# Sigmoid attention and a squared-ReLU feed-forward layer on one core: the scores of whole key chunks become native float32 products in quarters of the TensorE array

## The chip, the cores and the metric

The kernel runs on one core of one Trainium2 chip. The metric is the device time of one execution in microseconds (us), taken as the median over several runs. The engines spoken of are PE (TensorE, which multiplies matrices), PEld (its loading of the stationary operand, the "weights" of a product), DVE (VectorE), ACT (ScalarE) and SP (SyncE, which here only issues DMA transfers).

## The reference

`q`, `k`, `v` have 8 batches, 12 heads, 448 positions and 64 numbers per head; the feed-forward layer has 768 inputs and 2048 hidden units. All numbers are float32.

```python
def _attn_ref(q, k, v):
    S = q.shape[2]
    scale = 1.0 / np.sqrt(q.shape[-1])
    scores = scale * np.matmul(q, k.transpose(0, 1, 3, 2)) - np.log(S)
    attn = 1.0 / (1.0 + np.exp(-scores))
    return np.matmul(attn, v).astype(np.float32)

def _moe_ref(x, w_in, w_out, s, b):
    h = x @ w_in
    r = np.maximum(h, 0.0)
    g = s * (r * r) + b
    return (g @ w_out).astype(np.float32)

def reference(**kwargs):
    ...
    attn_out = _attn_ref(**attn_kwargs)
    B, H, S, D = attn_out.shape
    x = np.ascontiguousarray(attn_out.transpose(0, 2, 1, 3)).reshape(B * S, H * D)
    return _moe_ref(x=x, **moe_kwargs)
```

## The kernel before

The program has two parts. The attention comes first and takes the first quarter of the time; the feed-forward layer follows. The feed-forward layer runs over seven groups of 512 tokens: the first one directly, the other six in two threes, each with fewer products and with sums of weights and activations that DVE and ACT make ahead of them. The change doesn't touch that part.

**Quads.** The attention is a loop over 24 quads: a batch `b` and a third `t` of the 12 heads, so four heads. They are numbered 0 to 23 here. The four heads lie as `i` (0 or 1) and a half `r` of the 128 partitions: rows 0 to 63 hold one head's 64 numbers, rows 64 to 127 the other's. The tile `qk` of a quad is 128 partitions by `[i, queries or keys, 448]`.

**Blocks of scores.** The 448 keys of a head are three whole chunks of 128 and a last one of 64. A block `(i, c)` holds the scores of one whole chunk for the two heads of `i`: keys on the 128 partitions of the output, 448 queries along the free axis, head `j` in bank `j` of a PSUM tile of two banks. A quad has six blocks. ACT makes one sigmoid (L647) of each. The last chunks of all four heads make a seventh tile, `psc_l` (L686), with two heads' 64 keys on each half of the partitions; it is made one quad ahead.

**Scores in three products.** Before the change a block is made of three products of rounded parts. `hi` is the number rounded to the format that TensorE multiplies in one pass (fp32r), `lo` is what is left; the products are hi\*hi, lo\*hi and hi\*lo (`PARTS`). The parts of a quad are made one quad ahead: ACT rounds queries and whole key chunks (`parts_hi`, L630) after the six sigmoids, and DVE subtracts (`parts_lo`, L424) after its other work of the quad. For the first two quads DVE makes both (`parts_dve`). The first two blocks of quad 0 are native float32 products of the half arrays (L671), since their parts would come too late. Each product uses 64 rows by 128 columns of the array, and the two heads of a block run side by side in the two halves.

**Attention times values.** In 23 of the 24 quads the products with `v` are native float32 products in quarters of the array (64 rows by 64 columns), four at a time (`quarters`, L729; the last chunk L741). A native float32 product is one instruction of the program and two MATMUL records in the trace, so four products are `x8`. Quad 22 has them over 128 rows by 64 columns (`attn_v`, L699).

**PSUM slots.** There are four slots of two banks. Blocks one, two, five and six and `psc_l` take turns in `turn` (0 and 1). Blocks three and four stand in `held` (2 and 3), where the two `pav` tiles of the quad before have stood, and where those of this quad will stand. `held` is reversed after each quad in quarters. What releases a `pav` tile at the end of a quad is a copy on ACT (L734), a copy on DVE (L754) and two additions on DVE (L421, one per `pav` tile), which wait for the last product of the quad (L741):

```python
    def quarters_store(b, t, pav, x, last):
        copy = nc.vector.tensor_copy(x[:, 0], pav[0][:, 1, :S])
...
        for i in range(2):
            add(x[:, i], x[:, i], pav[i][:, i, :S])
```

Before the change the third block that PE makes is `(1, 0)`, which needs the slot that the first addition frees, and the fourth is `(0, 2)`, which needs the second addition.

**Other work.** Beside this, DVE, ACT and SP prepare the weights of the feed-forward layer in pieces that are laid out over the quads by hand-set tables (`ticks`). Each engine takes its instructions strictly in the order in which the program emits them. SP's queue in a quad is: the store of the quad before (`xd`), the values of the next quad (`v`), queries and keys two quads ahead (`qk`, into the buffer that this quad's scores read), weights (`st`), sums (`wd`).

Of the kernel before, what the change touches and what calls it, by code (L numbers as in the profile page):

```python
# [12 lines left out]
F32R = mybir.dt.float32r  # L13
# [25 lines left out]
PARTS = ((0, 0), (0, 1), (1, 0))  # L39
# [9 lines left out]
LATER_SUMS = (2, 3)  # L49
LATER_DUE = ((30.0, 84.0), (86.0, 140.0))  # L50
ROLL = 7
TWO = range(1, 24)
ROOM = 1.8
ACT_JOBS, ACT_AHEAD = 1.75, 0.9
DVE_JOBS = 6.9
# [276 lines left out]
def sigmoid_attention_relu2_ffn(  # L332
# [10 lines left out]
    nc = tc.nc  # L343
    B, NQ, P, _, _, S = qk.shape
    D = v.shape[5]
    NF, _, DM = w_in.shape
# [14 lines left out]
    def pool(stack, name, bufs, side=None, space=None):  # L361
        kw = dict(side=side) if side else {}
        if space is not None:
            kw["space"] = space
        return stack.enter_context(
            tc.tile_pool(name=name, bufs=bufs, reuse_waits="tile", **kw)
        )
# [49 lines left out]
    def f32(ap):  # L417
        return ap.bitcast(F32)
# [4 lines left out]
    def sub(o, x, y):  # L423
        nc.vector.tensor_tensor(o, x, y, op=ALU.subtract)  # L424


    order = [f + h * NP for f in range(NP) for h in range(2)]
# [160 lines left out]
    ldv = pool(at, "ldv", 2)  # L588
    qkx = ExitStack()
    ld = pool(qkx, "ld", 2)  # L590
    hl = pool(qkx, "hl", 1)
    ps_qk = pool(qkx, "ps_qk", 1, space=PSUM)
    ps_av = pool(at, "ps_av", 1, space=PSUM, side="right")

    turn, held = [0, 1], [2, 3]

    def place(k, name):
        pl = ps_qk if k < 2 else ps_av
        return pl.tile([P, 2, 512], F32, tag=f"s{k}", name=name)

    half = (slice(0, D), slice(D, P))
    quads = [(b, t) for b in range(B) for t in range(NQ)]
    NL = len(quads)

    def load(b, t, first=False):
        x = ld.tile([P, 2, 2, S], F32, tag="qk", name=f"qk_{b}_{t}")
        if first:
            nc.sync.dma_start(x[:, 0, 1, :P], qk[b, t][:, 0, 1, :P])
            nc.scalar.dma_start(x[:, 0, 0], qk[b, t][:, 0, 0])
            nc.sync.dma_start(x[:, 0, 1, P:], qk[b, t][:, 0, 1, P:])  # L610
            nc.scalar.dma_start(x[:, 1, 0], qk[b, t][:, 1, 0])
            nc.sync.dma_start(x[:, 1, 1], qk[b, t][:, 1, 1])
        else:
            nc.sync.dma_start(x, qk[b, t])
        return [x]
# [3 lines left out]
        nc.sync.dma_start(vt, v[b, t])  # L619
        ld_.append(vt)  # L620

    NX = S + 3 * P

    def flat(x):
        return x.rearrange("p i x s -> p i (x s)")[:, :, :NX]

    def parts_hi(b, t, ld_):

        hi, lo = (hl.tile([P, 2, NX], F32R, tag=h, name=f"qk{h}_{b}_{t}") for h in "hl")
        nc.scalar.copy(hi, flat(ld_[0]))  # L630
        ld_.append((hi, lo))

    def parts_lo(ld_):
        hi, lo = ld_[-1]
        sub(lo, flat(ld_[0]), f32(hi))

    def parts_dve(b, t, ld_, pieces):
        hi, lo = (hl.tile([P, 2, NX], F32R, tag=h, name=f"qk{h}_{b}_{t}") for h in "hl")
        x = flat(ld_[0])
        for i, cols in pieces:  # L640
            nc.vector.tensor_copy(hi[:, i, cols], x[:, i, cols])  # L641
            sub(lo[:, i, cols], x[:, i, cols], f32(hi[:, i, cols]))
        ld_.append((hi, lo))

    def sigmoid(psc, name):
        a = ap_.tile([P, 2, S], F32, tag="a", name=f"a_{name}")
        nc.scalar.activation(a, psc[:, :, :S], AF.Sigmoid, bias=nls, scale=SCALE)  # L647
        return a

    def scores(b, t, ld_):  # L650
        x = ld_[0]
        two = ld_.pop() if len(ld_) > 2 else None
        whole = two is None or (b, t) == quads[0]
        a = {}
        psc = {}
        order = [(i, c) for i in range(2) for c in range(3)]
        if not whole:
            order[2:4] = order[3], order[2]
        for k, (i, c) in zip(turn + (held[::-1] if whole else held) + turn, order):
            o = psc[i, c] = place(k, f"psc_{b}_{t}_{i}_{c}")  # L660
            if two and (i or c == 2 or not whole):
                cols = slice(S + c * P, S + (c + 1) * P)
                for m, (wi, xi) in enumerate(PARTS):
                    for j, r in enumerate(half):
                        nc.tensor.matmul(  # L665
                            o[:, j, :S], two[wi][r, i, cols], two[xi][r, i, :S],
                            start=m == 0, stop=m == 2,
                        )
            else:
                for j, r in enumerate(half):  # L670
                    nc.tensor.matmul(  # L671
                        o[:, j, :S], x[r, i, 1, c * P : (c + 1) * P], x[r, i, 0, :],
                        start=True, stop=True,
                    )
            if not whole and (i, c) == (1, 0):
                continue
            for k in [(i, c)] + [(1, 0)] * (not whole and (i, c) == (0, 2)):
                a[k] = sigmoid(psc[k], f"{b}_{t}_{k[0]}_{k[1]}")
        return a

    def scores_last(b, t, ld_, k):
        x = ld_[0]
        psc = place(k, f"psc_{b}_{t}_l")
        for j, r in enumerate(half):
            for i in range(2):
                nc.tensor.matmul(  # L686
                    psc[half[i], j, :S], x[r, i, 1, 3 * P :], x[r, i, 0, :],
                    start=True, stop=True,
                )
        return sigmoid(psc, f"{b}_{t}_l")  # L690
# [70 lines left out]
    loaded = {0: load(*quads[0], first=True)}  # L761
# [23 lines left out]
    def ticks(n, part, upto=99.0):  # L785
        jobs = sorted(plan.pop((n, part), ()), key=lambda x: x[:2])
        while jobs and jobs[0][3] <= upto:
            upto -= jobs[0][3]
            jobs.pop(0)[2]()
        if jobs:  # L790
            plan[n, part] = jobs
# [53 lines left out]
    pieces = [(l, f + h * NQ4) for f in range(NQ4) for l in (1, 0) for h in range(4)]  # L845
# [3 lines left out]
    pieces, late = iter(pieces[:-LATE]), pieces[-LATE:]  # L849
# [54 lines left out]
    at_step(NL - 1, "END", 0, lambda: first_lo(1))  # L904
    at_step(NL - 1, "END", -1, lambda: (base_lo(0, 0, w1[0]), base_store(0, 0, w1[0])))

    parts_dve(*quads[0], loaded[0], [(0, slice(S)), (1, slice(S)), (0, slice(S + 2 * P, NX)), (1, slice(S, NX))])
    al = {}

    def last_scores(n):  # L910
        al[n] = scores_last(*quads[n], loaded[n], turn[n == 1])
        if n > 1:
            turn.reverse()

    in_quarters = [n for n in range(NL) if n == NL - 1 or act(n) <= ACT_JOBS and dve[n] <= DVE_JOBS]
    for n, (b, t) in enumerate(quads):
        if n:
            ticks(n, "DVE")
        a = scores(b, t, loaded[n])
        between = None  # L920
        if n == 0:
            parts_dve(*quads[1], loaded[1], [(i, slice(NX)) for i in range(2)])
            ticks(0, "DVE")
            firsts = []

            def between():
                firsts.append(scores_last(*quads[0], loaded[0], 0))
                ticks(0, "ACT", ACT_AHEAD)

        else:  # L930
            if n + 1 in TWO:
                parts_hi(*quads[n + 1], loaded[n + 1])
            if n in in_quarters:

                def between():
                    if n + 1 < NL:
                        last_scores(n + 1)
                    ticks(n, "ACT", ACT_AHEAD if n + 1 < NL else 2.4)

            else:  # L940
                ticks(n, "ACT", ROOM)
        if n + 2 < NL:
            loaded[n + 2] = load(*quads[n + 2])
        ticks(n, "SP")
        for fn in stores:
            fn()
        stores.clear()
        if n == NL - 1:
            qkx.close()
            ps_h = pool(blk_ps, "ps_h", 2, space=PSUM)  # L950
        pav = (quarters if n in in_quarters else attn_v)(b, t, loaded[n], a, between)
        last = al[n] if n else firsts[0]
        if n + 1 < NL and n + 1 not in al:
            last_scores(n + 1)
        ticks(n, "ACT")
        if n in in_quarters:
            q_last = quarters_last(loaded[n], last, *pav)
        else:
            attn_v_last(loaded[n], last, pav)
        if n and n + 1 in TWO:  # L960
            parts_lo(loaded[n + 1])
        ticks(n, "END")
        if n in in_quarters:
            quarters_store(b, t, *pav[:2], q_last)
        else:
            store_x(b, t, pav)
        if n + 2 < NL:
            load_v(*quads[n + 2], loaded[n + 2])
# [365 lines left out]
    for a, *_ in PRODUCTS_1:  # L1334
        seen = [a]
        while seen:
            x = seen.pop(0)
# [178 lines left out]
    o = plan1.op("SP", 0.0, readers, opened, late=OPEN_DUE)  # L1516
# [3 lines left out]
    x = None  # L1520
    for k in range(AHEAD):
        _, l, row, p = stream[k]
        after = [o, x] + [row_op.get((l, row, f)) for f in (2 * p, 2 * p + 1)]
        x = plan1.op("SP", 1.28, after, lambda at: fetch(), late=OPEN_DUE + 6.0 + 2.8 * k)
# [84 lines left out]
```

## Time and profile before

| what | before |
|---|---|
| time, median of 3 runs | 1014.2 us (1013.45 to 1015.75) |
| span of the profiled execution | 1011.5 us |
| what lies around the span (median less span) | 2.7 us |
| attention, from the start to the first product of the feed-forward layer | 246.6 us |
| busy share of the span: PE, DVE, ACT | 100%, 88%, 72% |
| granted TensorE clock | 1.000 |

The profile is of one execution. Its span runs from the first to the last instruction; the timed runs also count what lies around it, so a change of the span is added to the median. A busy PE is one with a product somewhere in its pipeline; it does not say that the products follow each other as closely as they can. That is read from the distance between the starts of products that follow each other.

### The profile page before, as it was taken

The numbers are of one execution on the slowest core, as the hardware profiler recorded it, in microseconds if no ns is written. First come the engines' busy times: TensorE is split into PE (matmuls) and PEld (weight loads), VectorE is DVE, ScalarE is ACT, GpSimd is POOL, SyncE is SP. The second block draws the span as 40 slices with busy tenths as digits, with TensorE's granted clock in tenths as the row PEclk, the third lists the DMA queues.
The fourth block names the chain that finished last, engine by engine and source line by source line (L and its number), as shares of the span: only waits on it lengthen the run. The fifth ranks groups of instructions, "written<-read, shape, count | busy, mean of one in ns | idle before, by whom it ended". The sixth has DMA issues, their size and how long they took to land.

```text
span 1011.5 us, 15098 instructions
## 1 busy us (share of the span) xinstructions
PE 1007.4 (100%) x5746; PEld 766.2 (76%) x5746; DVE 891.7 (88%) x1035; ACT 725.7 (72%) x795; POOL 0.2 (0%) x4
## 2 busy tenths in 40 slices
PE   9999999999999999999999999999999999999998
PEld 4555555556888888888888888888888888888887
DVE  5999999999999957999978999996668678899995
ACT  7999999999777756748999944424544979964430
POOL 0000000000000000000000000000000000000000
PEclk9999999999999999999999999999999999999999
DMA  8887999996998999998966666898776666666774
GB/s 304 306 317 273 357 340 393 341 354 256 357 409 333 356 397 368 363 336 276 308 190 195 197 188 192 253 357 302 216 217 190 193 199 188 191 200 191 211 249 165
DMA packets 101080, 278.87 MB, mean 276 GB/s; under 512 B 10000, under 2 KB 23184, under 8 KB 101008
## 3 DMA queue, kind: packets, MB, share of 16 engines
q1 hardware_dynamic: 100720, 277.45, 80.1%
q8 instruction: 46, 0.75, 0.3%
q10 hardware_dynamic: 288, 0.46, 0.1%
q14 instruction: 26, 0.21, 0.1%
HBM read 193.99 MB, written 83.89 MB: 275 GB/s over the span
## 4 chain that ended last, share of the span: by engine, by line
PE 99%; DMA 0%; DVE 0%; issue 0%
PE b L1091 31%; PE b L1100 31%; PE pav L729 11%; PE psc L665 9%; PE ph L881 6%; PE po L1353 6%; PE psc_l L686 2%; PE pav L741 2%; PE pav L699 0%; DMA qk<-qk_t 0%; PE o L1114 0%; DVE qkl L424 0%; DVE qkh L641 0%; PE pav L708 0%; DVE r L424 0%
## 5 line engine op out<-in xcount | busy, mean ns | idle before, releaser
L1091 PE MATMUL b<-o_0h,wu 128*128 128x512 f32 x928 | 286.1, 389 | 0.0
L1091 PEld LDWEIGHTS b<-o_0h,wu 128*128 128x128 f32 x928 | 174.2, 188 | 36.1
L1091 PE MATMUL b<-o_0l,wu 128*128 128x512 f32 x464 | 180.5, 389 | 0.0
L1100 PE MATMUL b<-o_0h,wu 128*128 128x512 f32 x464 | 152.2, 389 | 0.0
L1100 PE MATMUL b<-o_1h,wu 128*128 128x512 f32 x456 | 149.6, 389 | 0.0
L647 ACT ACTIVATE a<-psc,nls 128x896 f32<-128x896 f32 x144 | 132.9, 1009 | 7.8 <-PE psc L665 5.5
L729 PE MATMUL pav<-a,v 64*64 64x448 f32 x1104 | 113.0, 540 | 0.0
L421 DVE TENSOR_TENSOR r<-r,b 128x1024 f32<-128x1024 f32 x74 | 89.4, 1215 | 24.4 <-PE b L1091 19.1
L1091 PEld LDWEIGHTS b<-o_0l,wu 128*128 128x128 f32 x464 | 87.1, 188 | 18.0
L1100 PEld LDWEIGHTS b<-o_0h,wu 128*128 128x128 f32 x464 | 87.1, 188 | 18.1
L1100 PEld LDWEIGHTS b<-o_1h,wu 128*128 128x128 f32 x456 | 85.7, 188 | 17.7
L424 DVE TENSOR_TENSOR r<-r,b 128x1024 f32<-128x1024 f32 x66 | 79.9, 1215 | 20.4 <-PE b L1100 11.8
L1100 PE MATMUL b<-o_0l,wu 128*128 128x512 f32 x232 | 90.2, 389 | 0.0
L1100 PE MATMUL b<-o_1l,wu 128*128 128x512 f32 x228 | 88.7, 389 | 0.0
L729 PEld LDWEIGHTS pav<-a,v 64*64 64x64 f32 x1104 | 40.0, 133 | 58.8 <-issue 46.2
L1041 ACT CAST o_0h<-r 128x1024 fp32r<-128x1024 f32 x26 | 27.4, 1052 | 57.2 <-DVE r L424 35.3
L1146 ACT ACTIVATE r<-b 128x1024 f32<-128x1024 f32 x46 | 46.3, 1027 | 30.2 <-DVE r L421 12.8
L1353 PE MATMUL po<-g,w 128*128 128x512 f32 x288 | 67.7, 389 | 0.0
L494 ACT CAST t<-t 128x768 fp32r<-128x768 f32 (+2 forms) x62 | 44.7, 734 | 29.1 <-DVE t L424 19.6
L1353 PEld LDWEIGHTS po<-g,w 128*128 128x128 f32 x288 | 54.1, 188 | 11.2
L881 PE MATMUL ph<-x0h,w 128*128 128x512 f32 x192 | 61.6, 390 | 0.0
L1220 ACT ACTIVATE r<-r,b_sb,s_sb 128x1024 f32<-128x1024 f32 x48 | 59.5, 1242 | 1.0
(122 smaller groups left out, 1728.2 us busy)
## 6 DMA issues: line engine op xcount, KB each, us to landing
wu<-wd SPq DMA_DIRECT2D x232, 512.0 KB, 3.6
wd<-t SPq DMA_DIRECT2D x36, 768.0 KB, 7.6
qk<-qk_t SPq DMA_DIRECT2D x23, 896.0 KB, 7.1
st<-w_out SPq DMA_DIRECT2D x16, 768.0 KB, 8.8
st<-w_in SPq DMA_DIRECT2D x16, 768.0 KB, 8.5
wd<-t SPq DMA_DIRECT2D x22, 512.0 KB, 4.8
v<-v_t SPq DMA_DIRECT2D x24, 448.0 KB, 5.7
xd<-xo SPq DMA_DIRECT2D x24, 448.0 KB, 3.5
```

The source lines that it names most:

```text
L421: nc.vector.tensor_tensor(o, x, y, op=ALU.add)
L424: nc.vector.tensor_tensor(o, x, y, op=ALU.subtract)
L494: nc.scalar.copy(ts[g][:, :n, 0], f32(ts[g][:, :n, 1]))
L647: nc.scalar.activation(a, psc[:, :, :S], AF.Sigmoid, bias=nls, scale=SCALE)
L665: nc.tensor.matmul(o[:, j, :S], two[wi][r, i, cols], two[xi][r, i, :S], start=m == 0, stop=m == 2,)
L729: nc.tensor.matmul(o[r, m, :S], ld_[1][rows, 3 * i + c, j, :], a[i, c][rows, j, :], start=c == 0, stop=c == 2 and m != i,)
L881: nc.tensor.matmul(ph, w[:, k, wi, kc * P : (kc + 1) * P], x0[h][xi][:, cc, :], start=m == 0, stop=m == 3 * NCC - 1,)
L1091: nc.tensor.matmul(bk[:, j], wt[:, j, wi, c * P : (c + 1) * P], tiles[xi][:, c, :], start=first and m == 0, stop=m == 3 * KC - 1, skip_gro ...
L1100: nc.tensor.matmul(bk[:, e], wt[:, f, wi, e * P : (e + 1) * P], tiles[gi][:, f], start=first and f == 0 and m == 0, stop=p == np_ - 1 and ...
L1146: nc.scalar.activation(v.t, bank_t[b], AF.Copy, scale=-1.0)
L1220: nc.scalar.activation(v.t, v.t, AF.Identity, bias=b_sb, scale=s_sb)
L1353: nc.tensor.matmul(pos[e], w[:, k, wi, kc * P : (kc + 1) * P], g[:, gi, :], start=first and i == 0, stop=last and i == 2,)
```

## The change

All whole-chunk scores are made as `psc_l` already is: native float32 products in quarters of the array, straight from `qk`. A block is four products of 64 rows (a head's numbers) by 64 columns (half of the chunk's keys). The parts of queries and keys, their pool `hl` and their instructions on ACT and DVE go. The order of blocks in a quad is now always `(0,0) (0,1) (0,2) (1,0) (1,1) (1,2)`, and each sigmoid follows its block.

```diff
-TWO = range(1, 24)
...
-    def parts_hi(b, t, ld_):
-
-        hi, lo = (hl.tile([P, 2, NX], F32R, tag=h, name=f"qk{h}_{b}_{t}") for h in "hl")
-        nc.scalar.copy(hi, flat(ld_[0]))
-        ld_.append((hi, lo))
...
     def scores(b, t, ld_):
         x = ld_[0]
-        two = ld_.pop() if len(ld_) > 2 else None
-        whole = two is None or (b, t) == quads[0]
         a = {}
         psc = {}
         order = [(i, c) for i in range(2) for c in range(3)]
-        if not whole:
-            order[2:4] = order[3], order[2]
-        for k, (i, c) in zip(turn + (held[::-1] if whole else held) + turn, order):
+        for k, (i, c) in zip(turn + held[::-1] + turn, order):
             o = psc[i, c] = place(k, f"psc_{b}_{t}_{i}_{c}")
-            if two and (i or c == 2 or not whole):
-                cols = slice(S + c * P, S + (c + 1) * P)
-                for m, (wi, xi) in enumerate(PARTS):
-                    for j, r in enumerate(half):
-                        nc.tensor.matmul(
-                            o[:, j, :S], two[wi][r, i, cols], two[xi][r, i, :S],
-                            start=m == 0, stop=m == 2,
-                        )
-            else:
+            for m, keys in enumerate(half):
+                k0 = c * P + keys.start
                 for j, r in enumerate(half):
                     nc.tensor.matmul(
-                        o[:, j, :S], x[r, i, 1, c * P : (c + 1) * P], x[r, i, 0, :],
+                        o[keys, j, :S], x[r, i, 1, k0 : k0 + D], x[r, i, 0, :],
                         start=True, stop=True,
                     )
-            if not whole and (i, c) == (1, 0):
-                continue
-            for k in [(i, c)] + [(1, 0)] * (not whole and (i, c) == (0, 2)):
-                a[k] = sigmoid(psc[k], f"{b}_{t}_{k[0]}_{k[1]}")
+            a[i, c] = sigmoid(psc[i, c], f"{b}_{t}_{i}_{c}")
         return a
...
-            if n + 1 in TWO:
-                parts_hi(*quads[n + 1], loaded[n + 1])
...
-        if n and n + 1 in TWO:
-            parts_lo(loaded[n + 1])
```

On PE, the second to fourth block of quad 5 before the change. Names are `psc` (scores), then third of the heads, `i`, `c` and a buffer number; `qkh` and `qkl` are the parts.

```order
L665 MATMUL psc_2_0_1_784<-qkh_2_711 128x448 [waits Activation_49]
L665 MATMUL psc_2_0_1_784<-qkh_2_711 128x448
L665 MATMUL psc_2_0_1_784<-qkl_2_712,qkh_2_711 128x448 x2
L665 MATMUL psc_2_0_1_784<-qkh_2_711,qkl_2_712 128x448 x2
L665 MATMUL psc_2_1_0_793<-qkh_2_711 128x448 [waits DVE_49]
L665 MATMUL psc_2_1_0_793<-qkh_2_711 128x448
L665 MATMUL psc_2_1_0_793<-qkl_2_712,qkh_2_711 128x448 x2
L665 MATMUL psc_2_1_0_793<-qkh_2_711,qkl_2_712 128x448 x2
L665 MATMUL psc_2_0_2_800<-qkh_2_711 128x448 [waits DVE_49]
```

The same place after the change:

```order
L635 MATMUL psc_2_0_1_695<-qk_2_524 64x448 [waits Activation_49]
L635 MATMUL psc_2_0_1_695<-qk_2_524 64x448 x3
L635 MATMUL psc_2_0_2_702<-qk_2_524 64x448 [waits DVE_49]
L635 MATMUL psc_2_0_2_702<-qk_2_524 64x448 x3
L635 MATMUL psc_2_1_0_709<-qk_2_524 64x448 x4
```

A block was six products of 128 output rows and is four of 64 (`x4`, or one with a wait and `x3`). The third block now waits for DVE alone and the fourth for nothing more: its slot is freed by the first addition, the third's by the second addition.

On DVE, the end of quad 4 before the change (`xo` is the attention's output; `wf`, `st` and `t` are weights and their sums):

```order
L421 TENSOR_TENSOR t_0_0_652<-wf_12_115,wf_4_113 128x256
L445 TENSOR_SCALAR wf_8_100<-st_8_596 128x768 [waits DMAHW2_49]
L424 TENSOR_TENSOR qkl_2_712<-qk_2_594,qkh_2_711 128x1664 [waits DMAHW1_49,PE_49,Activation_49]
L754 COPY xo_1_718<-pav_1_0_719 128x448 [waits DMAHW7_49,PE_49]
L421 TENSOR_TENSOR xo_1_718<-xo_1_718,pav_1_0_719 128x448 [waits DVE_49,PE_49]
L421 TENSOR_TENSOR xo_1_718<-xo_1_718,pav_1_1_740 128x448 [waits PE_49,Activation_49]
```

The same place after the change:

```order
L420 TENSOR_TENSOR t_0_0_581<-wf_12_115,wf_4_113 128x256
L444 TENSOR_SCALAR wf_8_100<-st_8_526 128x768 [waits DMAHW2_49]
L715 COPY xo_1_632<-pav_1_0_633 128x448 [waits DMAHW7_49,PE_49]
L420 TENSOR_TENSOR xo_1_632<-xo_1_632,pav_1_0_633 128x448 [waits DVE_49,PE_49]
L420 TENSOR_TENSOR xo_1_632<-xo_1_632,pav_1_1_654 128x448 [waits PE_49,Activation_49]
```

The making of `lo` no longer stands between the weights' work and the copy. On ACT the 22 instructions of L630 go in the same way. On SP the order of the 513 rows stays; the load of `qk` waits for PE where it waited for ACT, since the last reader of its buffer is now the quad's sixth block. Behind the attention the order of every engine is as before.

## Rows read from the trace of the kernel before

**Rows 1.** The page's first part: busy us, share of the span, instructions.

```profile
PE 1007.4 (100%) x5746; PEld 766.2 (76%) x5746; DVE 891.7 (88%) x1035; ACT 725.7 (72%) x795; POOL 0.2 (0%) x4
```

**Rows 2.** Windows: attention, feed-forward part, quads 1 to 21; then granted clock, DMA share, GB/s.

```profile
0.00:246.60 246.60, 245.51 (x2381) 135.04 (x2381) 228.32 (x317) 234.68 (x260) 0.20 (x4) 1.00 0.88 326
246.60:1011.50 764.90, 761.88 (x3366) 631.12 (x3366) 663.37 (x719) 490.99 (x536) 0.00 (x0) 1.00 0.78 259
15.77:227.03 211.26, 211.25 (x2102) 117.80 (x2102) 203.00 (x277) 205.35 (x229) 0.00 (x0) 1.00 0.91 335
```

**Rows 3.** The chain that ended last, in order of time: start us, us, what.

```profile
15.77 3.84 PE psc L665 x36
...
49.77 2.44 PE pav L729 x24
52.21 0.75 PE psc_l L686 x8
52.97 2.25 PE pav L729 x24
55.22 0.75 PE pav L741 x8
55.97 3.86 PE psc L665 x36
...
227.03 3.85 PE psc L665 x36
230.88 4.67 PE pav L699 x24
...
237.22 3.93 PE psc L665 x36
...
246.59 8.38 PE ph L881 x36
```

**Rows 4.** Timeline of PE in quad 4: start us, us, instruction.

```profile
45.86 0.47 PE L665 MATMUL psc<-qkh 64*128 64x448 f32 x2
46.17 0.36 PE L665 MATMUL psc<-qkl,qkh 64*128 64x448 f32 x2
...
49.41 0.36 PE L665 MATMUL psc<-qkh,qkl 64*128 64x448 f32 x2
```

**Rows 5.** Timeline of PEld, quad 4: weight loads; idle before and who ended it.

```profile
47.04 0.19 PEld L665 LDWEIGHTS psc<-qkh 64*128 64x128 f32 x2
...
49.73 0.21 PEld L729 LDWEIGHTS pav<-a,v 64*64 64x64 f32 x8 [0.33 <-ACT a L647]
50.16 0.15 PEld L729 LDWEIGHTS pav<-a,v 64*64 64x64 f32 x4 [0.22 <-issue]
```

**Rows 6.** Timeline, quad 4: sigmoids on ACT, load of queries and keys on SP.

```profile
46.84 5.52 ACT L647 ACTIVATE a<-psc,nls 128x896 f32<-128x896 f32 x6
...
48.44 0.52 SPq L614 DMA_DIRECT2D qk<-qk_t  x1
```

**Rows 7.** Timeline of quad 0: half-array native products, and the last ones.

```profile
3.84 1.81 PE L671 MATMUL psc<-qk 64*128 64x448 f32 x8
...
14.84 0.93 PE L741 MATMUL pav<-a_l,v 64*64 64x448 f32 x8
```

**Rows 8.** Groups by line and form, attention: busy us, mean ns, idle before.

```profile
L424 DVE TENSOR_TENSOR qkl<-qk,qkh 128x1664 fp32r<-128x1664 f32 x22 | 41.5, 1888 | 1.9 <-ACT qkh L630 1.9
...
L630 ACT CAST qkh<-qk 128x1664 fp32r<-128x1664 f32 x22 | 35.1, 1595 | 0.0
```

**Rows 9.** Timeline of DVE: the additions after quad 0; quad 3's end and additions.

```profile
15.80 1.15 DVE L421 TENSOR_TENSOR xo<-xo,pav 128x448 f32<-128x448 f32 x2 [1.46 <-PE pav L741]
...
43.83 1.89 DVE L424 TENSOR_TENSOR qkl<-qk,qkh 128x1664 fp32r<-128x1664 f32 x1
...
46.36 1.15 DVE L421 TENSOR_TENSOR xo<-xo,pav 128x448 f32<-128x448 f32 x2
```

**Rows 10.** The page's DMA issues: KB each, median us to landing.

```profile
qk<-qk_t SPq DMA_DIRECT2D x23, 896.0 KB, 7.1
```

More of the change, by code (lines that the diff above doesn't have):

```diff
@@ L590, in sigmoid_attention_relu2_ffn @@
     ld = pool(qkx, "ld", 2)
-    hl = pool(qkx, "hl", 1)
     ps_qk = pool(qkx, "ps_qk", 1, space=PSUM)
@@ L620, in load_v @@
         ld_.append(vt)
-    NX = S + 3 * P
-    def flat(x):
-        return x.rearrange("p i x s -> p i (x s)")[:, :, :NX]
-    def parts_hi(b, t, ld_):
-        hi, lo = (hl.tile([P, 2, NX], F32R, tag=h, name=f"qk{h}_{b}_{t}") for h in "hl")
-        nc.scalar.copy(hi, flat(ld_[0]))
-        ld_.append((hi, lo))
[L633 to L643, printed above, removed]
     def sigmoid(psc, name):
@@ L905, in sigmoid_attention_relu2_ffn @@
     at_step(NL - 1, "END", -1, lambda: (base_lo(0, 0, w1[0]), base_store(0, 0, w1[0])))
-    parts_dve(*quads[0], loaded[0], [(0, slice(S)), (1, slice(S)), (0, slice(S + 2 * P, NX)), (1, slice(S, NX))])
     al = {}
@@ L921, in sigmoid_attention_relu2_ffn @@
         if n == 0:
-            parts_dve(*quads[1], loaded[1], [(i, slice(NX)) for i in range(2)])
             ticks(0, "DVE")
```

## The prediction

> **What bounds the kernel now.** I read the page's busy shares first: PE is busy for 1007.4 of 1011.5 us [rows 1]. That alone proves little, since a product counts as busy while it waits in the pipeline. So I read windows by stage: the attention takes 246.6 us, the rest 764.9, of which PE is busy 761.88; in quads 1 to 21 ACT (205.35 of 211.26) and DVE (203.00) are nearly as full as PE [rows 2]. It has to be asked whether PE waits for them. The chain of work that ended last, in order of time, runs from quad 1 to the feed-forward part over PE piece by piece, with no other engine between [rows 3]. The reader is to look at the distances between PE's starts, since they tell.
>
> A quad takes 211.26 / 21 = 10.06 us [rows 3]. It holds 18 pairs of parts products and eight blocks of native float32 quarter products (six with the values, one `psc_l`, one L741). From `psc_l` at 52.21 to the next quad at 55.97 stand five such blocks: 3.76 / 5 = **0.752 us each** [rows 3], whether they read `qk` or `a`. From the second to the eighteenth pair are 49.41 - 46.17 = 3.24 us for 16 steps: **0.2025 us a pair** [rows 4]. A block is two rounds of four products started together, 0.376 us each; the weights of the next round load in 0.15 us of it, and the loads then idle 0.22 [rows 5]. So 18 x 0.2025 + 8 x 0.752 = 3.65 + 6.02 = 9.66 us, and 0.40 of the quad is left. It lies where the shape of the product changes. Going out of the scores, the last pair starts at 49.41 and would be through at 49.61, but the weights for L729 load at 49.73 and the next round starts at 50.16, 0.43 later, not 0.376 [rows 4, 5]: 0.12 + 0.05. Coming in, L741 starts at 55.22 and is through 0.75 later, when the chain has the next quad begin; inside quad 4 the first pair takes 46.17 - 45.86 = 0.31, not 0.20 [rows 3, 4], and about 0.1 more passes before it.
>
> **Which of the two readings of these gaps.** The row puts the gap at 49.73 down to a sigmoid [rows 5]: six sigmoids from 46.84 in 5.52 us are 0.92 each, so the third ended at about 49.6 and just freed the slot of `pav` [rows 6]. But `psc_l`, L729 and L741, which have waits too, follow each other with no gap at all [rows 3]. So I take 0.35 of the 0.40 for the change of shape, which goes, and 0.05 for that wait, which goes too, since the scores will end later than the sigmoids' third. The Trainium skill, "TensorEngine Tiling (Array Packing)", section "Key Properties", says that changing the tiling mode drains TensorE, though changing the tile doesn't. By that rule the gaps go, as the seams inside the native part show in the trace. If they belonged to the waits and stayed, the sum below would be larger by up to 0.40 x 22 = 9 us.
>
> **The change, part by part.**
> (1) Scores. Six blocks a quad at 0.752 are 4.51 us in place of 3.65 and the 0.40 of gaps: a quad becomes 14 x 0.752 = 10.53, **+0.47 us**. Quads 1 to 21: 21 x 10.53 - 211.26 = +9.8. The price comes from `psc_l`, which has the same operands and shape [rows 3].
> Quad 22 keeps its products of 128 rows: 4.51 + (237.22 - 230.88) - (237.22 - 227.03) = 4.51 + 6.34 - 10.19 = +0.66 [rows 3]. Quad 23: 13 x 0.752 - (246.59 - 237.22) = 9.78 - 9.37 = +0.41 [rows 3].
> (2) Quad 0. PE starts with two native blocks at 3.84 [rows 7] and then waits for DVE's parts. Without them it has 15 blocks in a row. The first load costs 0.13: two blocks are recorded as 1.81, one as 0.93 (L741), and 1.81 - 0.93 - 0.75 = 0.13 [rows 7]. So 3.84 + 15 x 0.752 + 0.13 = 15.25, against 15.77 [rows 3, 7]: **-0.5**. If the data of `i` = 1 land late, this half microsecond is at stake and little more.
> (3) Parts. ACT loses 22 x 1.6 = 35.1 us, DVE 41.5 [rows 8], all of it beside PE: worth nothing by itself. If their cover were what held PE, quads would differ with their weights' work; what they give is slack, which (4) needs.
> (4) The third block's slot. It now waits for the second addition of the quad before, where it waited for the first. Queued behind that block on PE is everything. After quad 0, where DVE stood waiting, the additions began at 15.80 and ended at 16.95; L741's two rounds ended at 14.84 + 0.75 = 15.59 [rows 7, 9]. So the slot is free 1.36 after the quad's start, and its weights load some 0.05 later, at 1.41 (in quad 4 the two additions ran 1.15 from 46.36, so the first ended a little behind the middle, 46.94, and the third block's weights loaded at 47.04 [rows 5, 9]). The round is due at 2 x 0.752 = 1.50. A load that comes late has cost a round 0.05 [rows 5], so 0.09 of lead is enough: I take 0. The other bound: if DVE were as late as now, when `lo` runs until 45.7 and the additions end at 47.51, 1.65 after the start at 45.86 [rows 4, 9], the load comes at 1.70 and a quad loses 0.25: 22 x 0.25 = +5.5. DVE loses 1.89 us a quad [rows 8] and the quad grows by 0.47, so its copy comes well before L741's end; that is why I choose the low end.
> (5) SP. The load of `qk` waits for the sixth block, 4.7 us after the quad's start in place of 48.44 - 45.86 = 2.6 [rows 4, 6], and the weights' loads queue behind it. It lands 7.1 us later [rows 10], at 11.8; its first reader, the `psc_l` of the next quad, comes at 10.5 + 6.8 = 17.3. The 5.5 us between hide it; without them each us late would cost 22 us in all. Sigmoids keep 0.92 for blocks that now come every 0.752, and the fifth block needs the first sigmoid by 3.0, done by 2.0 [rows 4, 6].
> (6) The rest. The 764.9 us of the feed-forward part [rows 2] keep their order and PE their bound; nothing can be given back there.
>
> Sum: -0.5 + 9.8 + 0.66 + 0.41 = **+10.4 us**. On the profile's span: 1011.5 + 10.4 = 1021.9. The median of the runs is 2.7 above that span (1014.2), so **1024.6 us**. A difference under 0.2% (2 us) couldn't be told from none.
>
> **Rivals.**
> A, the third block waits for DVE's additions, (4)'s upper bound: DVE's work is made to fill a quad, and ACT, full as it is, feeds it; that speaks for it. Against it: 1.89 us leave DVE in each quad. 1024.6 + 5.5 = 1030.1.
> B, the gaps stay, because they are waits and not shape: +9 at most; with half of them 1029. Seams without a gap inside the native part speak against it [rows 3].
> C, the weights of the new order come out from under the rounds. In the new order of a block's quarters the row half changes fastest, in `psc_l` and the values the column half does; if a round couldn't start before its loads, each of 12 rounds a quad would lose 0.15 [rows 5]: 24 x 1.8 = 43, 1068 us. Two halves of rows side by side did run in step in quad 0 [rows 7], and quarters in step everywhere else. The Trainium skill, "TensorE: Matmul & The Clock Gate", section "The mechanism", says that weight loads overlap running products only when the row group differs. By that rule the loads of L729 would stand between rounds; here they lie inside them [rows 5], so the trace disagrees.
> D, the other side: not slower. Only a cheaper block does it, since the floor is PE's: a quad stays at 10.06 if a block takes (10.06 - 6.02) / 6 = 0.674 us. Both column quarters of a head now read the same queries, which no quarter product of before does; were they streamed once for both, a block might be shorter. The half-array products of quad 0 do exactly that over 128 columns and still took the 0.376 us a round [rows 7]. With 0.674 or less the time is 1014 or lower.
>
> **How the numbers follow.** My forecast 0.68, A 0.14 (with lesser forms of it), B 0.07, C 0.04, D 0.03; 0.04 for what I don't see. The likeliest alone would lie in 1023 to 1027. The range takes in A and half of B upward, and 2 us of runs' scatter and a smaller step downward: 1022 to 1030.5, with 0.13 outside above (C, the worst of A and B) and about 0.06 below. Faster by over 0.2%: 0.02; within: 0.02; slower: 0.96.
>
> **What would show it.** In the chain after, psc pieces of 4.5 us (x48) in place of 3.85 (x36), then pav of 2.25 with no 0.19 on top; quads 10.5 us apart; quad 1 starting near 15.3; the feed-forward part still 765 us. ACT near 690 us busy, DVE near 845. PE's weights idle before a psc block on "DVE xo" would mean A; a pav piece of 2.44, B; rounds longer than 0.38 in psc alone, C; shorter than 0.34, D. I would be wrong altogether if ACT or DVE, not PE, set the 10.06 us of a quad.

## The result and the profile after

The changed kernel takes 1025.3 us (median of 4 runs, 1025.1 to 1026.1) against 1014.0 (1013.5 to 1015.8): 1.0113 times as long, 95% interval 1.0101 to 1.0125. That is 11.4 us more; 10.4 were forecast, and 1024.6 us. The profiled execution took 1026.1 us, its span 1023.9 us.

The page's first part after, which answers to [rows 1]:

```profile
PE 1019.5 (100%) x6038; PEld 726.9 (71%) x6038; DVE 845.1 (83%) x1001; ACT 696.8 (68%) x773; POOL 0.2 (0%) x4
```

DVE has lost 47 us and ACT 29, and the kernel is slower: their work lay beside PE. The windows of the attention, the feed-forward part and quads 1 to 21 (columns as in [rows 2]):

```profile
0.00:257.58 257.58, 256.81 (x2672) 96.03 (x2673) 181.51 (x282) 204.13 (x236) 0.20 (x4) 1.00 0.87 313
257.58:1023.90 766.32, 762.65 (x3370) 630.84 (x3366) 663.60 (x719) 492.67 (x538) 0.00 (x0) 1.00 0.78 259
16.05:237.04 220.99, 220.99 (x2358) 82.88 (x2352) 165.14 (x256) 178.41 (x208) 0.00 (x0) 1.00 0.90 320
```

Quads 1 to 21 take 220.99 / 21 = 10.52 us each (forecast 10.53). But the feed-forward part takes 1.4 us more than before (1.3 by the starts of the products below), which was not forecast. The chain that ended last, quad 1 and the start of quad 2:

```profile
16.05 4.51 PE psc L635 x48
20.56 2.25 PE pav L690 x24
22.82 0.75 PE psc_l L647 x8
23.57 2.25 PE pav L690 x24
25.83 0.75 PE pav L702 x8
26.58 4.51 PE psc L635 x48
```

Against [rows 3] the reader sees 4.51 for six blocks in place of 3.84, and 2.25 for the first `pav` in place of 2.44: the 0.19 is gone, and the scores are 6 x 0.752 = 4.51 with no gap at their start.

For the rest, one table is enough. From PE's timeline of every kernel it takes the start of the first product of quad 1, of quad 22, of quad 23, of the first feed-forward piece (`ph`) and of the second (`po`), and gives the distances (us):

| kernel | quad 1 starts | quads 1 to 21, each | quad 22 | quad 23 | piece 1 | from there to the end |
|---|---|---|---|---|---|---|
| before | 15.70 | 10.06 | 10.19 | 9.37 | 8.29 | 756.7 |
| after | 15.88 | 10.52 | 10.83 | 9.88 | 9.60 | 756.7 |
| swap | 15.20 | 10.52 | 10.87 | 9.88 | 8.81 | 756.7 |
| halves | 15.76 | 10.89 | 11.04 | 10.13 | 8.30 | 756.7 |
| parts_unread | 15.62 | 10.52 | 11.88 | 9.88 | 8.88 | 756.8 |
| parts_swapped | 16.52 | 10.52 | 11.18 | 9.88 | 9.13 | 756.7 |
| late_add | 15.97 | 11.02 | 11.33 | 9.88 | 10.08 | 756.8 |
| slot9 | 16.02 | 10.52 | 10.83 | 9.88 | 8.29 | 757.0 |
| tiny | 16.39 | 10.52 | 10.82 | 9.88 | 8.29 | 756.7 |
| again | 16.57 | 10.52 | 10.83 | 11.27 | 8.30 | 756.7 |
| before_again | 16.30 | 10.06 | 10.25 | 9.38 | 8.34 | 756.7 |
| before_tiny | 15.96 | 10.07 | 10.24 | 9.38 | 9.36 | 756.7 |

Between the two profiled spans: +0.18 (quad 0), +9.73, +0.64, +0.51, +1.31, in all 12.4 us. Two entries differ from the forecast by more than 0.15 us: quad 0 (+0.18, not -0.5) and piece 1 (+1.31, not 0).

### The profile page after: what moved, and what is told of

The parts are those of the page before. It is cut to its first block, busy times and chain, and to the rows that moved or that the text cites. A ratio compares the mean times of both kernels' runs of the same rounds, so it can differ in the third digit from the quotient of the medians.

```text
span 1023.9 us, 15584 instructions
## 1 busy us (share of the span) xinstructions
PE 1019.5 (100%) x6038; PEld 726.9 (71%) x6038; DVE 845.1 (83%) x1001; ACT 696.8 (68%) x773; POOL 0.2 (0%) x4
## 4 chain that ended last, share of the span: by engine, by line
PE 98%; ACT 1%; issue 0%; DVE 0%; DMA 0%; ACTq 0%
PE b L1046 31%; PE b L1055 31%; PE psc L635 10%; PE pav L690 10%; PE po L1308 6%; PE ph L842 6%; PE psc_l L647 2%; PE pav L702 2%; PE pav L660 0%; PE idle L731 0%; PE o L1069 0%; DMA wd<-t 0%; ACT t L493 0%; DVE w L423 0%; ACT w L549 0%
## 5 line engine op out<-in xcount | busy, mean ns | idle before, releaser
L635 PE MATMUL psc<-qk 64*64 64x448 f32 x1152 | 113.1, 539 | 0.0
L635 PEld LDWEIGHTS psc<-qk 64*64 64x64 f32 x1152 | 40.1, 133 | 69.0 <-issue 49.8
L420 DVE TENSOR_TENSOR xo<-xo,pav 128x448 f32<-128x448 f32 x46 | 26.5, 618 | 54.5 <-PE pav L702 54.4
```

Of the source, the lines that this page charges most:

```text
L420: nc.vector.tensor_tensor(o, x, y, op=ALU.add)
L635: nc.tensor.matmul(o[keys, j, :S], x[r, i, 1, k0 : k0 + D], x[r, i, 0, :], start=True, stop=True,)
```

## The experiments

**Shape or wait.** `halves` makes the same whole products in half arrays.

```diff
-            for m, keys in enumerate(half):
-                k0 = c * P + keys.start
-                for j, r in enumerate(half):
...
-                        o[keys, j, :S], x[r, i, 1, k0 : k0 + D], x[r, i, 0, :],
...
+            for j, r in enumerate(half):
...
+                    o[:, j, :S], x[r, i, 1, c * P : (c + 1) * P], x[r, i, 0, :],
...
```

> The changed kernel with its whole-chunk scores in half-array products (64x128 keys, 448 queries), still native float32 and still from the whole numbers; nothing else differs. Theory (the shape): the 0.40 us a quad that the change gave back stood where a product of another array shape follows, so with halves before and quarters behind them the quad is 10.52 + 0.40 = 10.92 us again, 23 quads make +9, and the time is 1034 us; the rounds themselves stay at 0.376 us. Rival (the waits): the gaps came from waits on DVE's and ACT's parts, which this kernel has not got either, and the time stays at 1025 us, quads at 10.52.

Measured: 1033.0 us, ratio to before 1.0189 [1.0175, 1.0203]. The chain of `halves`, a quad and the next one's scores:

```profile
37.60 4.71 PE psc L633 x24
42.31 2.42 PE pav L688 x24
44.73 0.75 PE psc_l L645 x8
45.48 2.25 PE pav L688 x24
47.73 0.75 PE pav L700 x8
48.48 4.71 PE psc L633 x24
```

The scores cost 4.71 and not 4.51, the `pav` behind them 2.42 and not 2.25. Together 0.37 us a quad come back (0.40 were expected, and 1034 us), with no parts in the kernel and no engine to wait for but those of the changed kernel. So the gaps that [rows 4, 5] showed belong to the change of shape. This agrees with the rule of the Trainium skill, "TensorEngine Tiling (Array Packing)", section "Key Properties", on the draining at a change of mode.

**The order of the quarters.** `swap` exchanges the loops over `m` and `j`.

```diff
-            for m, keys in enumerate(half):
-                k0 = c * P + keys.start
-                for j, r in enumerate(half):
+            for j, r in enumerate(half):
+                for m, keys in enumerate(half):
+                    k0 = c * P + keys.start
```

> The changed kernel with the two loops inside a block exchanged, so that two products that follow each other share their rows of the array and no longer their columns. Theory (a round is four quarters that run together, whatever their order): rounds of 0.376 us, loads of 0.14 us inside them, 1025 us. Rival (a weight load can't slip beside a product on the same rows): in each round one or two of the 0.14 us loads stand in the open, 288 rounds, so +20 to +40 us or 1045 to 1065 us.

Measured: 1025.4 us (1024.3 to 1026.5), ratio 1.0113 [1.0099, 1.0126]; a quad takes 10.52 us. Rival C falls: a round is four quarters together in either order, and no load comes out from under it.

**The parts themselves.** `parts_unread` makes `hi` and `lo` again, and nobody reads them; `parts_swapped` does so too and takes the third and fourth blocks in the order of before. Against the changed kernel, in the loop over the quads:

```diff
+            if n + 1 in TWO:
+                parts_hi(*quads[n + 1], loaded[n + 1])
...
+        if n and n + 1 in TWO:
+            parts_lo(loaded[n + 1])
```

> The changed kernel with the parts made again by ACT and DVE as before (35.1 and 41.5 us of work), but read by nobody: the scores are the changed kernel's quarters. Theory 1 (the parts cost nothing, and neither does leaving them out): 1025 us. Theory 2 (DVE's lateness decides): DVE's two additions come 0.50 to 1.65 us after the quad's start as before instead of 0.22 to 1.37, the third block's load stands at 1.70 us where it is due at 1.50, each quad is 0.2 to 0.25 us longer and the time is 1030 us.

> As parts_unread (parts made and read by nobody, scores in quarters), and the third and fourth blocks in the order of the kernel before, so that the block whose slot DVE's additions free comes fourth and is due 2.25 us after the quad's start. Theory 1 (the parts cost nothing): 1025 us, as parts_unread. Theory 2 (the third block's slot decides): 1025 us here and 1030 us in parts_unread. If both are at 1030 us, ACT's work is what delays, by the sigmoids.

Measured: 1025.65 us (1.0116 [1.0102, 1.0130]) and 1024.2 us (1.0105 [1.0092, 1.0119]), quads of 10.52 us in both. In these 21 quads the parts cost nothing and their absence gives nothing. Theory 2 was wrong in its premise: in a quad of 10.52 us DVE makes `lo` early enough, and its additions wait for PE as without the parts. Once they were late: quad 22 of `parts_unread` took 11.88 us, and by the chain its third block waited there for DVE's additions, behind a `lo` that ran until 237.27, 0.66 us into the quad. In `parts_swapped` it took 11.18 us, where by the chain products of the scores also waited behind a late `lo`; in the changed kernel it takes 10.83.

**The third block's slot.** `late_add` puts a DVE copy of 0.62 us, read by nobody, between the two additions.

```diff
-        for i in range(2):
-            add(x[:, i], x[:, i], pav[i][:, i, :S])
+        add(x[:, 0], x[:, 0], pav[0][:, 0, :S])
+        spare = ap_.tile([P, S], F32, tag="spare", name=f"spare_{b}_{t}", bufs=1)
+        nc.vector.tensor_copy(spare, pav[0][:, 0, :S])
+        add(x[:, 1], x[:, 1], pav[1][:, 1, :S])
```

> The changed kernel with one more DVE copy (128x448 out of PSUM, 0.62 us, read by nobody) between the two additions that store a quad, so that the slot of the next quad's third block comes free 0.62 us later. Theory (the third block's slot is nearly due: its load stands 1.42 us after the quad's start, the block 1.50): 0.08 us of slack are used up, and 0.54 us stand open in each of the 21 quads that follow a quad in quarters, +11 us or 1036 us, and in the trace a wait of PE on DVE ahead of the third block. Rival (the block has more room than the forecast gave it, because the quad's later work takes it up): 1025 us.

Measured: 1036.7 us (1.0226 [1.0212, 1.0240]), and 0.50 us more in each quad. First the changed kernel's timeline at quad 4, whose first round starts at 47.45, then that of `late_add` at quad 4, whose first round starts at 49.06:

```profile
47.67 1.15 DVE L420 TENSOR_TENSOR xo<-xo,pav 128x448 f32<-128x448 f32 x2 [2.58 <-PE pav L702]
48.87 0.23 PEld L635 LDWEIGHTS psc<-qk 64*64 64x64 f32 x8 [0.52 <-DVE xo L420]
49.34 0.14 PEld L635 LDWEIGHTS psc<-qk 64*64 64x64 f32 x4 [0.23 <-issue]
```

```profile
49.06 1.68 PE L635 MATMUL psc<-qk 64*64 64x448 f32 x16
49.82 0.62 DVE L720 COPY spare<-pav 128x448 f32<-128x448 f32 x1
50.35 0.61 DVE L420 TENSOR_TENSOR xo<-xo,pav 128x448 f32<-128x448 f32 x1
51.01 0.21 PEld L635 LDWEIGHTS psc<-qk 64*64 64x64 f32 x8 [1.04 <-DVE xo L420]
51.44 0.15 PEld L635 LDWEIGHTS psc<-qk 64*64 64x64 f32 x4 [0.22 <-issue]
```

In the changed kernel the additions end 1.37 us after the quad's start (47.67 + 1.15 - 47.45) and the load stands at 1.42: forecast 1.36 and 1.41. The wait for DVE is in the trace (0.52 in front of the load), but it costs nothing, because the round is due at 1.50 and what is behind it comes on time. In `late_add` the second addition ends at 50.96, 1.90 after the start: the copy takes 0.62, but its end overlaps the next instruction, so the slot comes free only 0.53 later. The load then stands at 1.95, 0.45 behind the due time of 1.50, and the round after it loads 0.43 later and not 0.376, which is the 0.05 of a late load from (4): together the 0.50. So the slack is 0.53 - 0.45 = 0.08, where 0.09 was forecast. Rival A is real, and 0.08 us away.

**Piece 1.** `x0l` are the first tokens of the feed-forward part and `x0h` their cast by ACT, each in two halves; they take slots of the eight in the rotating buffer `cx`. Timeline of the changed kernel there:

```profile
251.60 0.37 SPq L537 DMA_DIRECT2D wd<-t  x1
254.18 0.87 ACT L549 CAST w<-wf 128x768 fp32r<-128x768 f32 x1
257.40 1.48 ACT L856 CAST x0h<-x0l 128x1536 fp32r<-128x1536 f32 x1 [2.35 <-issue]
258.90 1.76 DVE L423 TENSOR_TENSOR x0l<-x0l,x0h 128x1536 fp32r<-128x1536 f32 x1 [2.87 <-ACT x0h L856]
260.72 0.50 PE L842 MATMUL ph<-x0l,w 128*128 128x512 f32 x1 [0.58 <-DVE x0l L423]
```

PE waits for DVE, DVE for the cast, and the cast 2.35 us for something the row doesn't name. In the program it is the store of row sums (`wd`) issued at 251.60, whose slot the second cast takes. The DMA view from its issue on says why it was late; first before, 240.9 to 244.6, then after, 251.5 to 257.4:

```profile
GB/s 0 0 0 0 0 0 0 0 0 0 221 509 399 399 376 399 399 443 443 421 376 376 421 399 465 421 376 376 421 376 399 89 0 177 0 0 0 0 0 0
...
wd<-t SPq DMA_DIRECT2D x1, 768.0 KB, 3.5
```

```profile
GB/s 0 0 0 0 0 0 83 472 389 333 417 361 403 417 375 347 389 375 403 320 42 0 14 14 0 28 28 28 28 28 28 14 28 28 28 28 14 347 417 417
...
q8 instruction: 1, 0.02, 2.1%
...
wd<-t SPq DMA_DIRECT2D x1, 768.0 KB, 5.7
```

Before, the store runs through at some 400 GB/s, and one instruction packet of 16 KB follows it (the 177 near the end). After, the packet falls into the store, at 252.63 us for 1.94 us, and what is left of the store comes at 14 to 28 GB/s for 2.3 us: about what one of 16 DMA engines moves, 400 / 16 = 25. The profile names neither the engine nor whose code the queue q8 carries, but its packets go with TensorE's instructions: 48 in the whole program where there are 6038 loads and as many products, 43 in `halves` with 5462, one for some 250 in both. The change has 292 products more than before, so its packets stand elsewhere against the work. Three kernels test the two links. `slot9` unties the cast from the store, `tiny` moves the packets earlier, `before_tiny` moves them into the store in the kernel before.

```diff
-    cx = Slots(pool(first, "cx", 1), 8, "c")
+    cx = Slots(pool(first, "cx", 1), 9, "c")
```

> The changed kernel with nine slots instead of eight in the rotating buffer that holds tokens, cast tokens and row sums, so that the cast of the second half of the first tokens takes a slot that is long free and waits no more for the store of the row sums of quad 23. Theory (this store lands late and holds the cast, the cast holds DVE and the first feed-forward piece): first piece 8.3 us again instead of 9.6, 1024.0 us. Rival (the first piece waits for ACT's or DVE's own work): 9.6 us stay, 1025.3 us.

```diff
-    for _ in range(WARM):
+    for _ in range(WARM - 4):
         nc.tensor.matmul(idle[:, 0, :S], ones[:, :P], ones[:, :S], start=True, stop=True)
+    for _ in range(32):
+        nc.tensor.matmul(idle[:32, 0, :8], ones[:, :32], ones[:, :8], start=True, stop=True)
```

> The changed kernel with four of the eight idle warm-up products replaced by 32 tiny ones (32x8), which adds 56 instructions to TensorE's stream ahead of all else and moves each 16 KB packet of its instructions about 2.6 us earlier against the work. Theory (the instruction packet at 252.63 us, 1.94 us long, ran into the store of the row sums and stretched its landing from 3.5 to 5.7 us): the packet falls ahead of the store, the store lands in 3.5 us, the first feed-forward piece takes 8.3 us instead of 9.6, 1024.0 us. Rival (the store is slow for another reason, as the writes to the same rows): it lands in 5 to 5.8 us as before, 1025.3 us. The four warm-up products less may let the clock rise later: up to 0.9 us in quad 0, to be read from the trace by itself.

> The kernel before with one of the eight idle warm-up products replaced by 13 tiny ones: 24 instructions more in TensorE's stream, which moves the 16 KB instruction packet that stood at 243.96 us about 1.2 us earlier, into the store of the row sums (its packets ran from 241.8 to 243.8 us). Theory (packet and store collide): the store lands in about 5 us instead of 3.5, the first feed-forward piece takes 8.9 to 9.6 us instead of 8.3, 1014.6 to 1015.3 us. Rival (no effect of the packet): 8.3 us and 1014.0 us.

Measured: `slot9` 1024.2 us (1.0103 [1.0089, 1.0117]), piece 1 8.29. `tiny` 1025.7 us (1.0117 [1.0104, 1.0131]), piece 1 8.29, with the packet at 251.00, ahead of the store; quad 0 gave part of the gain back, since its rounds ran at half speed until towards the end of the fourth, as in `again` below, and quad 1 started at 16.39. `before_tiny` 1014.9 us, 1.0010 [1.0001, 1.0019], piece 1 9.36, with the packet at 243.73 inside the store, 2.3 us after its issue where it came 3.0 after it before; its median is 1.3 us above that of the runs of before beside it (1013.7). The store in `tiny` and in `before_tiny`:

```profile
wd<-t SPq DMA_DIRECT2D x1, 768.0 KB, 3.8
```

```profile
q8 instruction: 1, 0.02, 1.1%
...
wd<-t SPq DMA_DIRECT2D x1, 768.0 KB, 5.1
```

Both links hold, and `before_tiny` shows that quarters have no part in it: the number of instructions ahead of the place is enough. The times alone would hardly settle 1 us; the table's column does, with one trace of each kernel.

**Quad 0.** `again` and `before_again` are the two kernels unchanged, for a second trace.

> The changed kernel once more, unchanged, for its trace. Theory (the 0.65 us by which quad 1 came later than forecast is the moment at which the clock rises in the first products, which differs from execution to execution): the first rounds step from about 0.75 to 0.376 us at another moment than 5.3 us, between 4.1 and 6.0 us as in the other traces, and quad 1 starts that much earlier or later than 15.88 us; the 21 quads behind it take 10.523 us each all the same. Rival (quarter products raise the clock later than half-array products do): the step at 5.3 us and quad 1 at 15.9 us again. The instruction packet lies within 0.7 us of where it lay, and the first feed-forward piece takes 8.8 us or more.

> The kernel before once more, unchanged, for its trace. Theory (the clock's rise moves from execution to execution): its first rounds may step to 0.376 us at another moment than 4.1 us, here too between 4.1 and 6.0 us, and quad 1 starts between 15.6 and 16.5 us. Rival (half-array products raise it early each time): the step at 4.1 us and quad 1 at 15.7 us again. Quads of 10.06 us and a first feed-forward piece of 8.3 us by both.

Measured: 1026.8 and 1014.0 us, one run each. Weight loads of quad 0 in after, then in `again`, then in `before_again`:

```profile
3.84 0.30 PEld L635 LDWEIGHTS psc<-qk 64*64 64x64 f32 x8 [0.73 <-DMA qk<-qk_t]
4.82 0.23 PEld L635 LDWEIGHTS psc<-qk 64*64 64x64 f32 x4 [0.67 <-issue]
5.36 0.14 PEld L635 LDWEIGHTS psc<-qk 64*64 64x64 f32 x4 [0.32 <-issue]
5.74 0.14 PEld L635 LDWEIGHTS psc<-qk 64*64 64x64 f32 x4 [0.23 <-issue]
```

```profile
4.64 0.25 PEld L635 LDWEIGHTS psc<-qk 64*64 64x64 f32 x4 [0.50 <-issue]
5.39 0.25 PEld L635 LDWEIGHTS psc<-qk 64*64 64x64 f32 x4 [0.50 <-issue]
6.14 0.25 PEld L635 LDWEIGHTS psc<-qk 64*64 64x64 f32 x4 [0.50 <-issue]
6.80 0.14 PEld L635 LDWEIGHTS psc<-qk 64*64 64x64 f32 x4 [0.42 <-issue]
```

```profile
4.75 0.34 PEld L671 LDWEIGHTS psc<-qk 64*128 64x128 f32 x2 [0.41 <-issue]
5.50 0.34 PEld L671 LDWEIGHTS psc<-qk 64*128 64x128 f32 x2 [0.41 <-issue]
6.25 0.34 PEld L665 LDWEIGHTS psc<-qkh 64*128 64x128 f32 x2 [0.41 <-DVE qkl L424]
6.81 0.19 PEld L665 LDWEIGHTS psc<-qkl,qkh 64*128 64x128 f32 x2 [0.22 <-issue]
```

The first rounds stand 0.75 us apart (5.39 to 6.14) and later 0.376, and a load takes 0.25 us and later 0.14. So I take it that TensorE begins at the lower of its two levels, 1.2 GHz, and steps to 2.4 while it works. This rests on that factor of about two alone: the granted-clock column reads 1.00 from the start. Ahead of them stand eight idle products from 0.77 us on, alike in all these kernels but the two tiny ones. The step came within the first round in `swap` (whose loads stand at 4.35, 4.68 and 5.06), after two rounds in after, towards the end of the fourth in `again`, and as late in `before_again`, where the first trace of before had it early. So it goes by the execution, not by quarters or halves, and the rival falls; but in both new traces the step came later than the 4.1 to 6.0 us that were expected (behind the loads at 6.14 and 6.25). The Trainium skill, "TensorE: Matmul & The Clock Gate", section "What's actually happening", says that this moment isn't tied to the kernel's start and differs from run to run; the traces agree.

`again` missed in two more things. The packet came at 255.13 and not within 0.7 us of 252.63: the store, issued at 252.29, was by then all but through and landed in 3.3 us. And piece 1 took 8.30, but quad 23 11.27 us. There the first cast waited for a store of row sums issued at 236.41, at the end of quad 21, 11.54 us from issue to landing in the chain; the sigmoid `a_l` behind it came late, and PE stood in quad 23's scores. It is the same wait on a slot, at another store and another cast.

## Why the prediction was right

**Scores (1).** Right to a hundredth of a us in each of the 21 quads. A block of whole-number quarters costs what `psc_l` costs, so a quad holds 14 blocks of 0.752; +9.73 in quads 1 to 21 where +9.8 was forecast, +0.64 in quad 22 where +0.66. Quad 23 gave +0.51, not +0.41: 13 x 0.752 leaves out the step to the first feed-forward product, 257.58 against the end of the last round at 256.72 + 0.75 = 257.47, which before had too.

**The gaps.** Put down to shape and not to waits, and `halves` brought 0.37 of the 0.40 back. Rival B falls.

**The parts (3).** Worth nothing, as forecast: making them again changed no quad of the 21. DVE's busy time is the 845 us forecast; ACT's is 696.8 where near 690 was forecast, which cost PE nothing.

**The slot (4).** The choice of the low bound was right for the reason given: DVE waits for PE (2.58 us ahead of the additions) and is no longer late. The forecast of load and due time held within 0.01, and that of the lead, 0.09, by `late_add` (0.08).

**SP (5).** In quad 4 the load of `qk` went out at 52.20, 4.75 us after the start (forecast 4.7), landed 6.8 us later (median), and nobody waited for it.

**Rival D** had no chance: rounds stay at 0.376.

**Quad 0 (2): the size was off.** -0.5 holds where the clock steps up early: `swap` starts quad 1 at 15.20, before at 15.70. The forecast took the early step of before's trace as a fixed part of the program. It missed that the change takes cover away: before, PE waited in quad 0 for DVE's parts anyway, so a late step cost `before_again` only 0.60 (16.30 - 15.70), while without the waits it costs 1.37 (16.57 - 15.20). With late steps in both the change loses 0.27 there.

**The rest (6): one sentence failed.** "Nothing can be given back there" looked at PE's order and not at what its code does to the DMA queues. From `po` on the 756.7 us are the same in nearly every trace, but the first piece was 1.31 us longer in the profiled run, and of the other kernels with 6038 products those with the slot and the start unchanged lost 0.5 to 1.8 there or, in `again`, ahead of it. In the profiled run quad 0 and piece 1 stand 0.70 and 1.31 us above the forecast. The median of the runs stands 0.7 above it; `slot9`, which has no such wait, has 1024.2. That it is only 0.7 is in part luck, since the 2.7 us around the span were too much: 2.2 lie between time and span in each of the four runs of the changed kernel, and 1.7 to 1.8 in every later run of the kernel before. By spans, 1021.9 was forecast and 1022.9 to 1023.9 came, a median 1.2 above. How much of it is quad 0 in the runs without a profile can't be read, since they have no trace.

No variant here beats the kernel before. `slot9` has a median 1.1 us below the changed one's, which the times alone don't settle (the intervals 1.0089 to 1.0117 and 1.0101 to 1.0125 overlap), and is still 1% behind: quarters of whole numbers cost 0.86 us a quad more than three products of parts (4.51 against 3.65) and give back 0.40.

## What to carry to other kernels

Where one engine is full, price a change of product form by the row of a product of that form and shape that already runs, times its count, and price each change of shape between neighbours by itself (here 0.17 going out of the scores and 0.20 coming in); the work that other engines lose is worth nothing, unless a buffer's release hangs on it, and then its slack can be read (here 0.08 us). For differences of about 1 us, compare stage by stage over several traces: an instruction packet that meets a store, or a clock that steps up later, moves that much with no change in the work.

## What the hardware showed that was not expected

One 16 KB packet of code, by its count TensorE's, 0.9 to 1.9 us long, that falls into a 768 KB store stretches its landing to between 5.0 and 5.8 us (seven traces), where stores that met none took 3.3 to 3.8, with a tail at the rate of one of 16 DMA engines. Where it came as the store ended (`again`, 2.8 us after the issue), it cost nothing. Adding 24 instructions at the program's start did this to a stage 240 us later. And the first rounds, from 3.84 us on, ran at half speed for less than one round or for nearly four, by the execution, while the profile's granted clock showed 1.00; half speed is read from the rounds, 0.75 us apart and then 0.376.
